# A second `x` buffer in an attention and MLP kernel, and the mixing of a batch spread over three pairs

## The chip, the cores and the metric

The kernel runs on one core of a Trainium2 chip. It is written with five engines in mind: TensorE (PE, matrix products and transposes, with its weight loads shown as PEld), VectorE (DVE), ScalarE (ACT), GpSimd (POOL) and SyncE (SP, which issues all DMAs here). Each engine runs its own queue in order; semaphores order the queues against each other. The metric is the time of one execution on the device in microseconds, as the median of several runs.

## The reference

For each of 4 batches there are 8 heads of attention over 576 positions with a head dimension of 64, in float32:

```python
scores = (q @ k.T) / sqrt(64) + bias          # bias: (8, 576, 576), the same for all batches
attn = exp(scores - max) / (sum + 1e-9)
x[b] = concat over heads of (attn @ v)        # (576, 512)
```

The bias is a small network (hidden size 32, ReLU) of log1p|i - j| / log1p(max(i, 1)). Behind it comes a block on `x`:

```python
h = x.T @ U @ V                # U: 576 x 32, V: 32 x 576: mixes the positions of one batch
u = x + h.T
out = u + relu(u @ w_ch1) @ w_ch2      # w_ch1: 512 x 2048, w_ch2: 2048 x 512
```

The mixing (`x.T @ U @ V`) of a batch needs all heads and all positions of that batch's `x`. The MLP works on `u`, 2304 rows in all.

## The kernel before, in words

Attention runs over 16 pairs: pair p is batch p // 4 and two heads, numbered hp = p % 4. A pair has 9 slots (`slot(p, s)`, lines 504 to 534). Each slot computes one tile of scores, 128 rows by 576 (`scores`: TensorE products `sc`, then a VectorE instruction, line 321, that adds the bias and finds the row minimum), and its exponentials on ScalarE (`exps`, line 340). Slots 3 to 8 and, one pair later, slots 0 and 1 transpose the exponentials on TensorE (`tr`, tile `tb`; `tr_m`, tile `tm`; `tr_mid`, tile `ti`). ScalarE (line 367) or VectorE (line 369) copies each transposed bank into the SBUF tile `pt`: slots 4, 6 and 8 go to ScalarE, 3, 5 and 7 to VectorE, but in pairs with hp = 1 slots 3 and 5 go to ScalarE too (line 520). The PV product of the first half of the rows (`av`, tile `o`, line 423) stands at the end of slot 8; the one of the second half in slot 2 of the next pair. `assemble` transposes the results (tile `tx`) and VectorE writes them, scaled, into `x_sb` (lines 446 and 453): slot 4 of the next pair for the first half, slot 8 for the second.

All transposes and the mixing use PSUM tiles of tag "t". They are one bank each and come in turn from three banks (`psum`, line 77; `rot`, line 716). A use waits until the use three before it has been read out.

`x_sb` holds one batch's `x`, with one buffer. Its mixing runs in the first pair of the next batch whose hp is 1 (pairs 5, 9, 13), because the last `assemble` of the batch is in slot 8 of the pair before:

- `mix_t` (line 457), ahead of slot 0: `mt = U.T x` on TensorE, then `th` on ScalarE and `tl` on VectorE (a sum of two parts in a reduced format).
- `mix_s` (line 484), behind slot 0: `ms` from `th` and `tl`, then `sq` on ScalarE and again on VectorE.
- `mix_h` (line 495), behind slots 1 to 5, for the row blocks 4, 0, 1, 2, 3: a product `mh` with `sq`, a VectorE add into `x_sb` (line 499), and a DMA of the block to `u_dram` (line 500).

The `assemble` of the next batch's first pair in slot 4 writes the same `x_sb`, so it waits until those DMAs have read it. The last batch's mixing (lines 836 to 847) lies between the steps of the MLP.

Three more streams run beside the slots:

- Loads and splits of q and k. `load_pair(p + 2)` is issued on SP at the start of slot 7 into `raw`, which has one buffer. POOL splits it into `hi` and `lo` (lines 155 and 161, four instructions) in slots 2 to 5 of the next pair, for the pair after that.
- The conversion of the 64-bit MLP weights (`conv_ops`, lines 175 to 212; `background`, line 664), one step in each of the slots 0, 1, 2, 6, 7, 8 from pair 2 on: load, two ScalarE steps, two VectorE steps (lines 193 and 199), a join on VectorE (line 205) with an add on POOL (line 210), a store. With three steps a job, and the order fixed, the joins stand in slots 0 and 6 of pairs 3 to 12.
- From pair 13 on the first MLP weights are loaded and split; in slots 6 and 7 of pair 15 `make_ut` adds one use of a "t" bank each (transposes `tu`).

Ahead of all this, a bias phase uses tables in the pool `tabp` (5 KB a partition), which stay allocated until the MLP although nothing reads them after it.

Of the kernel before, what the change touches and what calls it, by code (L numbers as in the profile page):

```python
# [8 lines left out]
F32 = mybir.dt.float32  # L9
F32R = mybir.dt.float32r  # L10
# [8 lines left out]
B, H, S, D = 4, 8, 576, 64  # L19
HP = H // 2  # L20
DM = H * D
# [4 lines left out]
P = 128  # L26
# [20 lines left out]
def kernel(  # L47
# [14 lines left out]
    nc = tc.nc  # L62
# [10 lines left out]
    p0 = ExitStack()  # L73
# [3 lines left out]
    def psum(tag, shape, name):  # L77
        rot[tag].append(rot[tag].pop(0))
        return rot[tag][-1].tile(shape, F32, tag=tag, name=name)
# [7 lines left out]
    p1 = ExitStack()  # L87
    mix = p1.enter_context(tc.tile_pool(name="mix", bufs=1, side="left"))
# [13 lines left out]
    u_sb = mix.tile([P, 5, RANK], F32, name="u_sb")  # L102
    vq = mix.tile([P, 640], F32R, name="vq")
    fold = mix.tile([P, P], F32R, name="fold")
    x_sb = mix.tile([P, 5, DM], F32, name="x_sb")

# [22 lines left out]
    def load_pair(p):  # L131
        b, hp = divmod(p, HP)
        raw = rawp.tile([P, QKW], F32, tag="raw", name="raw")
        nc.sync.dma_start(out=raw[0:D], in_=qk[b, hp])
        nc.sync.dma_start(out=raw[D:P], in_=qk[b, hp])
        qk_ops[p] = raw

    def load_v(p):
        b, hp = divmod(p, HP)
        v_t[p] = vpp.tile([P, 640], F32, tag="v", name="v")  # L140
        nc.sync.dma_start(out=v_t[p], in_=vp[b, hp])
# [70 lines left out]
        return load, [size, low, clamp, shift, join, add], lambda: finish(st["y"].bitcast(F32))  # L212


    tabp = p1.enter_context(tc.tile_pool(name="tabp", bufs=1, side="left"))
    ring = [big.tile([P, 9 * S], F32, tag=f"big{i}", name="ring") for i in (2, 3)]
    ring = [t[:, i * S : (i + 1) * S] for t in ring for i in range(9)]

# [63 lines left out]
            parts = [(bias[hp][t * LEFT : (t + 1) * LEFT, 0:S], bd[4 * P : S, 2 * hp + t, :]) for t in range(2)]  # L282
        return [lambda o=o, i=i: nc.sync.dma_start(out=o, in_=i) for o, i in parts]


    pools = {}

    pair = {}

    def new_pair(p):  # L290
        st = stp.tile([P, 32], F32, tag="st", name="st")
        pair[p] = {"st": st, "P": {}}
# [72 lines left out]
    def copy(eng, out, in_):  # L365
        if eng == "a":
            nc.scalar.copy(out=out, in_=in_)  # L367
        else:
            nc.vector.tensor_copy(out, in_)  # L369
# [64 lines left out]
    def assemble(p, hf):  # L434
        d = pair[p]
        ot = d["ot", hf]
        hp = p % HP
        bank = psum("t", [P, 4, P], "tx")
        o = LEFT if hf == 0 else 0
        for i in range(2):  # L440
            nc.tensor.transpose(bank[:, i, :], ot[:, o + i * P : o + (i + 1) * P], ident)
        if hf == 0:
            nc.tensor.transpose(bank[0:LEFT, 2, :], ot[:, 0:LEFT], ident)
        xs = x_sb[:, 2 * hf : 2 * hf + 2, hp * P : (hp + 1) * P].rearrange("p c (h d) -> p c h d", h=2)
        r = d["st"][:, 21 + 4 * hf : 25 + 4 * hf].rearrange("p (c h) -> p c h", h=2)
        nc.vector.tensor_tensor(
            out=xs,
            in0=bank[:, 0:2, :].rearrange("p c (h d) -> p c h d", h=2),
            in1=r.unsqueeze(3).to_broadcast([P, 2, 2, D]),
            op=ALU.mult,  # L450
        )
        if hf == 0:
            copy("d", x_sb[0:LEFT, 4, hp * P : (hp + 1) * P], bank[0:LEFT, 2, :])
# [2 lines left out]

    def mix_t(b):

        t = psum("t", [P, DM], "mt")
        for c in range(4):  # L460
            mm(
                t[RANK * c : RANK * (c + 1), :],
                lhsT=u_sb[:, c, :],
                rhs=x_sb[:, c, :],
                start=True,
                stop=False,
                tile_position=(0, RANK * c),
            )
        for g in range(4):
            mm(  # L470
                t[RANK * g : RANK * (g + 1), g * P : (g + 1) * P],
                lhsT=u_sb[:, 4, :],
                rhs=x_sb[:, 4, g * P : (g + 1) * P],
                start=False,
                stop=True,
                tile_position=(0, RANK * g),
            )
        th = mix.tile([P, DM], F32R, tag="th", name="th")
        tl = mix.tile([P, DM], F32R, tag="tl", name="tl")
        nc.scalar.copy(out=th, in_=t)  # L480
        nc.vector.tensor_tensor(out=tl, in0=t, in1=th.bitcast(F32), op=ALU.subtract)
        mixt[b] = (th, tl)

    def mix_s(b):

        th, tl = mixt[b]
        s = psum("t", [P, DM], "ms")
        mm(s, lhsT=fold, rhs=th, start=True, stop=False)
        mm(s, lhsT=fold, rhs=tl, start=False, stop=True)
        sq = mix.tile([P, DM], F32R, tag="sq", name="sq")  # L490
        nc.scalar.copy(out=sq, in_=s)
        nc.vector.tensor_tensor(out=sq[D:P], in0=s[D:P], in1=sq[D:P].bitcast(F32), op=ALU.subtract)
        mixt[b] = sq

    def mix_h(b, c):
        n = P if c < 4 else LEFT
        h = psum("t", [P, DM], "mh")
        mm(h, lhsT=vq[:, c * P : (c + 1) * P], rhs=mixt[b], start=True, stop=True)
        nc.vector.tensor_tensor(out=x_sb[0:n, c, :], in0=h[0:n], in1=x_sb[0:n, c, :], op=ALU.add)
        nc.sync.dma_start(out=u_dram[b * S + c * P : b * S + c * P + n, :], in_=x_sb[0:n, c, :])  # L500
# [167 lines left out]
        del queue[:n]  # L668


    pools["pt"] = p1.enter_context(tc.tile_pool(name="ptp", bufs=1, side="left"))
    nc.sync.dma_start(out=ident, in_=ident_in)
    nc.vector.memset(sgn.bitcast(F32), -2.0)
    nc.vector.memset(eps, 1.0e-9)
# [8 lines left out]
    for i in range(len(order) + 2):  # L683
# [23 lines left out]
            load_v({20: 0, 26: 1}[i])  # L707
        if i in early:
            slot(0, early[i])
    nc.vector.memset(x_sb[D:P, 4, :], 0.0)  # L710
    ones = tabp.tile([P, RANK], F32, name="ones")
    nc.vector.tensor_reduce(out=ones, in_=ident.rearrange("p (g r) -> p r g", g=4), op=ALU.add, axis=mybir.AxisListType.X)
    nc.vector.tensor_copy(fold.rearrange("p (g r) -> p g r", g=4), ones.unsqueeze(1).to_broadcast([P, 4, RANK]))
    p0.close()
    psT2 = ctx.enter_context(tc.tile_pool(name="psT2", bufs=2, space=PSUM))
    rot = {"s": [psS], "t": [psT, psT2, psT2]}
    loads[0:0] = bias_loads(3, 0)
# [7 lines left out]
    queue[1:1] = [[]] * 3  # L725

    conv_at = (0, 1, 2, 6, 7, 8)

    def big_views(t, parts):

        views, o = [], 0
        for n, k in parts:
            if k is None:
                o += n
                continue
            views.append(t[:, o : o + n].rearrange("p (k f) -> p k f", k=k) if k else t[:, o : o + n])
            o += n
        return views
# [12 lines left out]
    for p in range(NP):  # L751
        if p > 0:
            new_pair(p)
        if 0 < p < HP - 1:
            bias[p + 1] = big.tile([P, 9 * S], F32, tag=f"big{p + 1}", name=f"bias{p + 1}")
            loads = [o for c in (4, 0, 1, 2, 3) for o in bias_loads(c, p + 1)]
        for s in range(9):
            if s == (1 if p else 0) and p < NP - 1:
                prep = prep_ops(p + 1)
            if s in ((2, 3, 4, 5) if p else (0, 1, 2, 3)) and p < NP - 1:  # L760
                prep.pop(0)()
            if s == 7 and 0 < p < NP - 2:
                load_pair(p + 2)
            if s == 7 and 0 < p < NP - 1:
                load_v(p + 1)
            for o in loads[0:2]:
                o()
            del loads[0:2]
            if p > 0 or s not in early.values():
                if p > HP and p % HP == 1 and s == 0:  # L770
                    mix_t(p // HP - 1)
                slot(p, s)
                background(int(s in conv_at and (p, s) >= CONV_FROM))
                if p > HP and p % HP == 1 and s == 0:
                    mix_s(p // HP - 1)
            if p > HP and p % HP == 1:
                for c in {1: (4,), 2: (0,), 3: (1,), 4: (2,), 5: (3,)}.get(s, ()):
                    mix_h(p // HP - 1, c)
            if p == NP - 3 and s == 1:
                t = big.tile([P, 9 * S], F32R, tag="big0", name="w1q")  # L780
                *wq[0], uth[0] = big_views(t, [(WQ, KD), (WQ, KD), (LINE, None), (UT, KD)])
                feed = first_weights(0)
            if p == NP - 2 and s == 1:
                t = big.tile([P, 9 * S], F32R, tag="big1", name="w2q")
                w2a, w2b, utl[0] = big_views(t, [(WQ, KD), (WQ, KD), (LINE, None), (UT, KD)])
                wq[0] += [w2a, w2b]
                feed = first_weights(1)
            if p == NP - 1 and s == 1:
                t = big.tile([P, 9 * S], F32, tag="big2", name="acc")
                acc.update(enumerate(big_views(t, [(DM, 0)] * 10)))  # L790
                feed = iter(())
            if p >= NP - 3 and s in (1, 2, 4, 5, 7, 8):
                next(feed, None)
            if p == NP - 1 and s in (1, 2, 3, 4, 5):
                load_acc(2 * s - 2)
                load_acc(2 * s - 1)
            if p == NP - 1 and s in (6, 7):
                make_ut(0, s - 6)
# [155 lines left out]
```

## Time and profile before

| what | value |
|---|---|
| median of 3 runs | 774.79 us (770.87 to 774.82) |
| the profiled execution | 773.58 us, of which the span of instructions 771.7 us |
| TensorE busy | 738.4 us (96%) |
| VectorE, ScalarE, POOL busy | 437.4, 361.4, 235.8 us |
| chain that ended last | 72% TensorE |

The span goes from the first to the last instruction of the profiled execution; some 1.9 us of that execution lie outside it. Attention's pairs run from about 60 to 351 us, the MLP behind them. Instructions and stretches are placed by their time from the span's start. In a timeline or a table of stretches, "idle before" in square brackets is the time in which an engine stood still ahead of an instruction, with the instruction that ended it.

### The profile page before, as it was taken

The page shows a single profiled execution, that of the slowest core. Times are in us where ns is not written, and L with a number is a line of the kernel's source. Part 1 is how long each engine was busy: PE and PEld are TensorE (multiplying, and loading weights), DVE is VectorE, ACT ScalarE, POOL GpSimd, SP SyncE. Part 2 cuts the span into 40 slices and gives each one's busy share as a digit, 9 for nine tenths or more (in the row PEclk, how much of TensorE's full clock was granted, in tenths as well). Part 3 has the DMA queues.
Part 4 walks back from the last instruction along what each step waited for, and adds up shares of the span by engine and source line. Part 5 has one row for each costly group of instructions (what it writes and reads, how often), then busy time and mean ns, then how long its engine had stood idle before and what let it go on. Part 6 is the DMA issues. An engine that isn't in the chain of part 4 may idle for free.

```text
span 771.7 us, 13867 instructions
## 1 busy us (share of the span) xinstructions
PE 738.4 (96%) x5348; PEld 613.5 (80%) x5348; DVE 437.4 (57%) x949; ACT 361.4 (47%) x807; POOL 235.8 (31%) x225
## 2 busy tenths in 40 slices
PE   6989899999999998999999999999999999999998
PEld 4436777677867776878888889988998999999986
DVE  8995468868877885663439734762247722221222
ACT  7996577777777775774125513431114410111010
POOL 0004456655665566630005502540015500000000
PEclk9999999999999999999999999999999999999999
DMA  7898994465455546550063301320002200001111
GB/s 212 252 319 268 241 275 123 122 178 127 124 158 151 123 97 176 153 168 1 21 205 98 109 1 42 96 83 1 1 26 85 69 1 1 1 28 56 55 42 68
DMA packets 39377, 84.01 MB, mean 109 GB/s; under 512 B 6800, under 2 KB 9488, under 8 KB 37264
## 3 DMA queue, kind: packets, MB, share of 16 engines
q1 hardware_dynamic: 39312, 83.13, 37.0%
q8 instruction: 42, 0.69, 0.4%
q14 instruction: 23, 0.19, 0.1%
HBM read 60.96 MB, written 22.15 MB: 108 GB/s over the span
## 4 chain that ended last, share of the span: by engine, by line
PE 72%; ACT 8%; DVE 6%; DMA 5%; POOL 4%; issue 3%; SPq 1%; DVEq 0%; POOLq 0%; ACTq 0%
PE po L606 24%; PE ph L583 23%; PE o L423 8%; PE sc L319 7%; PE tb L387 4%; DMA raw<-in_qk_dram 3%; ACT ring L244 2%; DVE wt L205 1%; ACT ring L266 1%; PE bs L255 1%; POOL hi L161 1%; POOL lo L161 1%; DVE p L321 1%; POOL hi L155 1%; ACT p L340 1%
## 5 line engine op out<-in xcount | busy, mean ns | idle before, releaser
L588 ACT ACTIVATE hh<-ph 128x1024 fp32r<-128x1024 f32 x36 | 36.9, 1026 | 205.3 <-PE ph L583 205.3
L589 DVE SCALAR_TENSOR_TENSOR hh<-ph,hh 128x1024 fp32r<-128x1024 f32 x36 | 44.1, 1224 | 141.1 <-ACT hh L588 141.1
L340 ACT ACTIVATE p<-p,st 128x576 f32<-128x576 f32 x128 | 99.8, 780 | 41.3 <-DVE st L321 41.2
L210 POOL TENSOR_TENSOR wy<-wt,wy 128x256 int32<-128x256 int32 (+1 forms) x68 | 50.2, 738 | 217.8 <-DVE wt L205 195.9
L321 DVE CUSTOM_DVE_ANT_0 p<-sc,bias 128x576 f32<-128x576 f32 x128 | 95.9, 749 | 31.8 <-PE sc L319 26.6
L606 PE MATMUL po<-w2q,hh 128*128 128x512 f32 x432 | 101.8, 391 | 1.5 <-DVE acc L609 1.5
L606 PE MATMUL po<-wq,hh 128*128 128x512 f32 x432 | 103.2, 395 | 0.0
L319 PE MATMUL sc<-hi 128*128 128x288 f32 x320 | 101.6, 333 | 1.3 <-DVE st L321 0.8
L583 PE MATMUL ph<-ut,w1q 128*128 128x256 f32 x768 | 94.2, 280 | 0.0
L606 PEld LDWEIGHTS po<-w2q,hh 128*128 128x128 f32 x432 | 79.9, 188 | 17.9 <-issue 1.9
L606 PEld LDWEIGHTS po<-wq,hh 128*128 128x128 f32 x432 | 80.1, 188 | 17.6
L423 PE MATMUL o<-pt,v 128*64 128x320 f32 (+1 forms) x640 | 91.7, 412 | 2.1 <-ACT pt L367 2.1
L319 PE MATMUL sc<-lo,hi 128*128 128x288 f32 x320 | 90.7, 299 | 3.0 <-POOL lo L161 3.0
L583 PEld LDWEIGHTS ph<-ut,w1q 128*128 128x128 f32 x768 | 92.1, 188 | 1.5 <-issue 0.6
L583 PEld LDWEIGHTS ph<-ut,wq 128*128 128x128 f32 x768 | 90.3, 188 | 1.4
L583 PE MATMUL ph<-ut,wq 128*128 128x256 f32 x768 | 90.6, 277 | 0.0
L609 DVE TENSOR_TENSOR acc<-po,acc 128x512 f32<-128x512 f32 x72 | 49.6, 689 | 72.4 <-PE po L606 72.3
L387 PE MATMUL tb<-ident,p 128*128 128x128 f32 x512 | 78.2, 276 | 5.8 <-DVE x_sb L369 4.2
L423 PEld LDWEIGHTS o<-pt,v 128*64 128x64 f32 x640 | 45.2, 136 | 37.6 <-ACT pt L367 7.0
L319 PEld LDWEIGHTS sc<-hi 128*128 128x128 f32 x320 | 61.2, 191 | 15.1 <-issue 8.6
L387 PEld LDWEIGHTS tb<-ident,p 128*128 128x128 f32 x512 | 61.9, 142 | 8.3 <-issue 6.2
L155 POOL TENSOR_SCALAR hi<-raw 128x1216 fp32r<-128x1216 f32 x30 | 36.3, 1210 | 99.8 <-DMA raw<-in_qk_dram 90.6
(99 smaller groups left out, 1036.9 us busy)
## 6 DMA issues: line engine op xcount, KB each, us to landing
raw<-in_qk_dram SPq DMA_DIRECT2D x31, 608.0 KB, 7.9
wraw<-in_w_ch_dram SPq DMA_DIRECT2D x64, 256.0 KB, 2.6
bias_dram<-ring SPq DMA_DIRECT2D x36, 288.0 KB, 4.1
v<-in_vp_dram SPq DMA_DIRECT2D x16, 320.0 KB, 8.3
bias<-bias_dram SPq DMA_DIRECT2D x16, 288.0 KB, 4.5
acc<-u_dram SPq DMA_DIRECT2D x18, 256.0 KB, 4.9
out_dram<-acc SPq DMA_DIRECT2D x18, 256.0 KB, 2.0
bias<-bias_dram SPq DMA_DIRECT2D x16, 256.0 KB, 4.7
```

Source lines behind the costliest of these rows:

```text
L155: nc.gpsimd.tensor_scalar(out=hi[:, a:e], in0=raw[:, a:e], scalar1=1.0, scalar2=0.0, op0=ALU.mult, op1=ALU.add)
L210: nc.gpsimd.tensor_tensor(out=st["y"], in0=st["t"], in1=st["y"], op=ALU.add)
L319: mm(ps[:, a, 0:HALF], lhsT=hi[:, q0 : q0 + P], rhs=kk, start=(i == 0), stop=(i == n - 1))
L321: nc.vector.tensor_tensor_reduce(out=halves(dst), in0=ps[:, :, 0:HALF], in1=halves(bias[hp][:, s * S : (s + 1) * S]), scale=-0.125, scalar ...
L340: nc.scalar.activation(out=dst, in_=dst, func=AF.Exp, bias=st[:, s : s + 1], scale=-1.0, accum_out=st[:, 10 + s : 11 + s])
L387: nc.tensor.transpose(bank[:, kb, :], src[:, b0 + kb * P : b0 + (kb + 1) * P], ident)
L423: mm(o[hd * D : (hd + 1) * D, 0:n], lhsT=v[:, vb * D : (vb + 1) * D], rhs=pt[:, pb, :], start=(j == 0), stop=(j == 4),)
L583: mm(st["ps"][:, f, :], lhsT=w, rhs=u[:, k, :], start=(i == 0), stop=(i == 3 * KD - 1))
L588: nc.scalar.activation(out=hh[n], in_=st["ps"], func=AF.Relu)
L589: nc.vector.scalar_tensor_tensor(out=hl[n], in0=st["ps"], scalar=0.0, in1=hh[n].bitcast(F32), op0=ALU.max, op1=ALU.subtract)
L606: mm(ps, lhsT=h, rhs=w, start=(m == 0), stop=(m == 3 * FG - 1))
L609: nc.vector.tensor_tensor(out=a, in0=ps, in1=a, op=ALU.add)
```

## The change

`x` gets a second buffer. The list `xbuf` holds both; batch b uses `xbuf[b % 2]`. Its space is that of the bias tables: their pool `tabp` now belongs to the part that is closed after the bias phase, the pool `ptp` of the transposed exponentials is opened ahead of it, and the new pool `xp` takes the freed place. The rows of the new buffer that no batch writes are set to zero once. `sq` shares the place of `th`.

With the second buffer, the mixing of a batch no longer has to be finished before slot 4 of the pair it starts in. `mix_t` stays ahead of slot 0 of pairs 5, 9, 13; `mix_s` goes behind slot 2 of that pair, and the five `mix_h` behind slot 7 of that pair, slots 2 and 7 of the next, and slots 2 and 7 of the one after. The last batch's mixing is left where it was.

```diff
--- before.py
+++ after.py
@@ -102,7 +102,7 @@
     u_sb = mix.tile([P, 5, RANK], F32, name="u_sb")
     vq = mix.tile([P, 640], F32R, name="vq")
     fold = mix.tile([P, P], F32R, name="fold")
-    x_sb = mix.tile([P, 5, DM], F32, name="x_sb")
+    xbuf = [mix.tile([P, 5, DM], F32, name="x_sb")]
 
 
 
@@ -212,7 +212,8 @@
         return load, [size, low, clamp, shift, join, add], lambda: finish(st["y"].bitcast(F32))
 
 
-    tabp = p1.enter_context(tc.tile_pool(name="tabp", bufs=1, side="left"))
+    pools = {"pt": p1.enter_context(tc.tile_pool(name="ptp", bufs=1, side="left"))}
+    tabp = p0.enter_context(tc.tile_pool(name="tabp", bufs=1, side="left"))
     ring = [big.tile([P, 9 * S], F32, tag=f"big{i}", name="ring") for i in (2, 3)]
     ring = [t[:, i * S : (i + 1) * S] for t in ring for i in range(9)]
 
@@ -282,8 +283,6 @@
             parts = [(bias[hp][t * LEFT : (t + 1) * LEFT, 0:S], bd[4 * P : S, 2 * hp + t, :]) for t in range(2)]
         return [lambda o=o, i=i: nc.sync.dma_start(out=o, in_=i) for o, i in parts]
 
-
-    pools = {}
 
     pair = {}
 
@@ -434,7 +433,8 @@
     def assemble(p, hf):
         d = pair[p]
         ot = d["ot", hf]
-        hp = p % HP
+        b, hp = divmod(p, HP)
+        x_sb = xbuf[b % 2]
         bank = psum("t", [P, 4, P], "tx")
         o = LEFT if hf == 0 else 0
         for i in range(2):
@@ -456,6 +456,7 @@
 
     def mix_t(b):
 
+        x_sb = xbuf[b % 2]
         t = psum("t", [P, DM], "mt")
         for c in range(4):
             mm(
@@ -487,13 +488,14 @@
         s = psum("t", [P, DM], "ms")
         mm(s, lhsT=fold, rhs=th, start=True, stop=False)
         mm(s, lhsT=fold, rhs=tl, start=False, stop=True)
-        sq = mix.tile([P, DM], F32R, tag="sq", name="sq")
+        sq = mix.tile([P, DM], F32R, tag="th", name="sq")
         nc.scalar.copy(out=sq, in_=s)
         nc.vector.tensor_tensor(out=sq[D:P], in0=s[D:P], in1=sq[D:P].bitcast(F32), op=ALU.subtract)
         mixt[b] = sq
 
     def mix_h(b, c):
         n = P if c < 4 else LEFT
+        x_sb = xbuf[b % 2]
         h = psum("t", [P, DM], "mh")
         mm(h, lhsT=vq[:, c * P : (c + 1) * P], rhs=mixt[b], start=True, stop=True)
         nc.vector.tensor_tensor(out=x_sb[0:n, c, :], in0=h[0:n], in1=x_sb[0:n, c, :], op=ALU.add)
@@ -668,7 +670,6 @@
         del queue[:n]
 
 
-    pools["pt"] = p1.enter_context(tc.tile_pool(name="ptp", bufs=1, side="left"))
     nc.sync.dma_start(out=ident, in_=ident_in)
     nc.vector.memset(sgn.bitcast(F32), -2.0)
     nc.vector.memset(eps, 1.0e-9)
@@ -707,11 +708,13 @@
             load_v({20: 0, 26: 1}[i])
         if i in early:
             slot(0, early[i])
-    nc.vector.memset(x_sb[D:P, 4, :], 0.0)
+    nc.vector.memset(xbuf[0][D:P, 4, :], 0.0)
     ones = tabp.tile([P, RANK], F32, name="ones")
     nc.vector.tensor_reduce(out=ones, in_=ident.rearrange("p (g r) -> p r g", g=4), op=ALU.add, axis=mybir.AxisListType.X)
     nc.vector.tensor_copy(fold.rearrange("p (g r) -> p g r", g=4), ones.unsqueeze(1).to_broadcast([P, 4, RANK]))
     p0.close()
+    xbuf.append(p1.enter_context(tc.tile_pool(name="xp", bufs=1, side="left")).tile([P, 5, DM], F32, name="x_sb"))
+    nc.vector.memset(xbuf[1][D:P, 4, :], 0.0)
     psT2 = ctx.enter_context(tc.tile_pool(name="psT2", bufs=2, space=PSUM))
     rot = {"s": [psS], "t": [psT, psT2, psT2]}
     loads[0:0] = bias_loads(3, 0)
@@ -725,6 +728,7 @@
     queue[1:1] = [[]] * 3
 
     conv_at = (0, 1, 2, 6, 7, 8)
+    mix_at = {(1, 7): 4, (2, 2): 0, (2, 7): 1, (3, 2): 2, (3, 7): 3}
 
     def big_views(t, parts):
 
@@ -767,15 +771,15 @@
                 o()
             del loads[0:2]
             if p > 0 or s not in early.values():
-                if p > HP and p % HP == 1 and s == 0:
-                    mix_t(p // HP - 1)
+                b, hp = divmod(p, HP)
+                if b and (hp, s) == (1, 0):
+                    mix_t(b - 1)
                 slot(p, s)
                 background(int(s in conv_at and (p, s) >= CONV_FROM))
-                if p > HP and p % HP == 1 and s == 0:
-                    mix_s(p // HP - 1)
-            if p > HP and p % HP == 1:
-                for c in {1: (4,), 2: (0,), 3: (1,), 4: (2,), 5: (3,)}.get(s, ()):
-                    mix_h(p // HP - 1, c)
+                if b and (hp, s) == (1, 2):
+                    mix_s(b - 1)
+                if b and (hp, s) in mix_at:
+                    mix_h(b - 1, mix_at[hp, s])
             if p == NP - 3 and s == 1:
                 t = big.tile([P, 9 * S], F32R, tag="big0", name="w1q")
                 *wq[0], uth[0] = big_views(t, [(WQ, KD), (WQ, KD), (LINE, None), (UT, KD)])
```

## Rows read from the trace of the kernel before

**Rows 1.** The page's busy times, TensorE's entry (first of its line).
```profile
PE 738.4 (96%) x5348; PEld 613.5 (80%) x5348; DVE 437.4 (57%) x949; ACT 361.4 (47%) x807; POOL 235.8 (31%) x225
```

**Rows 2.** Stretches of pairs 5, 7, 8, 9, 11, 13: length, busy by engine, clock, DMA.
```profile
139.97:163.30 23.33, 19.92 (x150) 15.21 (x149) 18.48 (x45) 15.51 (x38) 16.35 (x14) 1.00 0.53 148
...
180.04:197.98 17.94, 16.97 (x128) 13.29 (x127) 14.85 (x40) 12.82 (x33) 10.17 (x9) 1.00 0.53 132
197.98:214.51 16.53, 16.53 (x128) 13.28 (x127) 12.85 (x36) 12.94 (x33) 9.67 (x8) 1.00 0.56 144
214.51:236.41 21.90, 19.58 (x150) 14.90 (x150) 16.93 (x45) 15.45 (x37) 14.16 (x10) 1.00 0.58 162
...
252.94:270.71 17.77, 16.90 (x127) 13.21 (x127) 14.69 (x38) 12.82 (x33) 9.35 (x9) 1.00 0.55 134
...
287.45:311.86 24.41, 20.67 (x150) 16.25 (x149) 14.65 (x38) 15.55 (x36) 15.68 (x11) 0.93 0.61 172
```

**Rows 3.** Waits of the whole span: total us, times, longest.
```profile
DVE x_sb L446 <- DMA u_dram<-x_sb: 6.0, 4, 2.3
...
PE mh L498 <- DVE sq L492: 4.2, 3, 1.5
PE tb L387 <- DVE x_sb L369: 4.2, 2, 2.4
```

**Rows 4.** Timeline of pair 5's mixing: start, length, engine, line, tile, [idle before].
```profile
142.81 0.41 PEld L461 LDWEIGHTS mt<-x_sb,u_sb 128*32 128x32 f32 x8 [0.49 <-DVE st L321]
...
149.89 0.47 PE L498 MATMUL mh<-sq,vq 128*128 128x512 f32 x1 [1.51 <-DVE sq L492]
...
153.13 0.50 PE L498 MATMUL mh<-sq,vq 128*128 128x512 f32 x1
...
153.47 0.29 PE L319 MATMUL sc<-hi 128*128 128x288 f32 x1
...
158.63 0.63 PE L387 MATMUL tb<-ident,p 128*128 128x128 f32 x4 [1.74 <-DVE x_sb L369]
```

**Rows 5.** Groups by line, VectorE, 130 to 300 us: busy us, mean ns.
```profile
L205 DVE SCALAR_TENSOR_TENSOR wt<-wraw,sgn,wt 128x256 int32<-128x256 int32 (+1 forms) x17 | 15.9, 936 | 0.3
...
L499 DVE TENSOR_TENSOR x_sb<-mh,x_sb 128x512 f32<-128x512 f32 (+1 forms) x11 | 7.5, 679 | 1.9 <-PE mh L498 1.9
```

**Rows 6.** Timeline of pair 7, slots 6 to 8.
```profile
196.75 0.49 DVE L205 SCALAR_TENSOR_TENSOR wt<-wraw,sgn,wt 128x256 int32<-128x256 int32 x1
...
197.45 0.60 PE L387 MATMUL tb<-ident,p 128*128 128x128 f32 x4
...
197.95 0.69 DVE L369 COPY pt<-tb 128x512 f32<-128x512 f32 x1
```

**Rows 7.** Timeline of pair 15, slot 7's copy and slot 8's transposes.
```profile
346.73 0.68 DVE L369 COPY pt<-tb 128x512 f32<-128x512 f32 x1
...
347.56 0.63 PE L387 MATMUL tb<-ident,p 128*128 128x128 f32 x4 [0.92 <-DVE pt L369]
```

**Rows 8.** Timeline of pair 6, slots 6 to 8, with POOL.
```profile
178.71 2.79 POOL L161 TENSOR_TENSOR lo<-raw,hi 128x1216 fp32r<-128x1216 f32 x1
178.80 2.97 DVE L205 SCALAR_TENSOR_TENSOR wt<-wraw,sgn,wt 128x256 int32<-128x256 int32 x1
...
179.51 0.60 PE L387 MATMUL tb<-ident,p 128*128 128x128 f32 x4
...
182.49 0.69 DVE L369 COPY pt<-tb 128x512 f32<-128x512 f32 x1
```

**Rows 9.** Timeline of the loads of `raw` (SP) and POOL's first split.
```profile
144.66 0.47 SPq L134 DMA_DIRECT2D raw<-in_qk_dram  x1
...
191.52 1.21 POOL L155 TENSOR_SCALAR hi<-raw 128x1216 fp32r<-128x1216 f32 x1 [2.51 <-DMA raw<-in_qk_dram]
...
217.42 0.47 SPq L134 DMA_DIRECT2D raw<-in_qk_dram  x1
```

**Rows 10.** Timeline of VectorE at pair 0's end.
```profile
69.06 0.76 DVE L321 CUSTOM_DVE_ANT_0 p<-sc,bias 128x576 f32<-128x576 f32 x1 [3.60 <-DMA bias<-bias_dram]
```

## The prediction

> **What bounds the kernel now.** I read the page's engine lines first, then the stretches by pair, the waits, and the timeline around the mixing. TensorE is busy for 96% of the span [rows 1], so time can be won only where it stands still or runs slowly. The change touches pairs 4 to 15. In the stretches, each cut from one pair's first PV product (slot 8) to the next pair's, a pair without mixing can run with no hole at all: pair 8 takes 16.53 us and TensorE is busy 16.53 us of it. The pairs that carry the mixing of the batch before (5, 9, 13) take 23.33, 21.90 and 24.41 us with 19.92, 19.58 and 20.67 us busy [rows 2]. The holes have two names in the waits: the first `mh` product waits for VectorE's `sq` (4.2 us in three), and slot 5's transposes wait for VectorE's copy into `x_sb` (4.2 us in two), which stands behind a wait for the transfer `u_dram<-x_sb` (6.0 us in four) [rows 3]. Pair 5's timeline shows both: 1.51 us ahead of the first `mh`, 1.74 us ahead of the `tb` transposes at 158.63 [rows 4]. That second wait is one for a PSUM bank. Transposes and mixing share three banks used in turn (tag "t"); with an `mh` put between, slot 5's transposes get the bank of `tx` three uses earlier, which VectorE had not emptied.
>
> **What the change takes away.** Mixing costs TensorE 19.58 - 16.53 = 3.05 us a batch wherever it stands [rows 2]; that moves and does not go. The holes of the mixing pairs are 3.41 + 2.32 + 3.74 = 9.47 us. The wait of the first mixing matmul for the last `assemble`, 0.49 us [rows 4], stays in each, since `mix_t` stays. `mix_s` goes two slots later and the first `mix_h` five slots after it, so `sq` is ready; `assemble` writes the other buffer, whose transfer left a batch ago. I take 9.47 - 1.5 = 8.0 us away. In pair 13 the granted clock was 0.93, part of the pair at 1.2 instead of 2.4 GHz, after a hole; the same matmuls took 20.67 instead of 19.58 us [rows 2]. If the hole goes, 1.1 us goes with it. Together 9.1 us.
>
> **What it adds.** Per batch, slot 2 of two pairs gets one `mh` behind its PV. VectorE is busy 12.85 of 16.53 us in pair 8 [rows 2] and gets no scores while that PV runs, so the add of 679 ns [rows 5] fits: cost 0, at most the add, 0.7 us each. `mix_h` also goes behind slot 7 in three pairs (5, 6, 7 and so on). There it uses one bank between slot 7's transposes and slot 8's two uses. Before, slot 8's `tb` takes the bank of slot 6's `ti`; after, it takes the bank of slot 7's `tb`, which VectorE copies. In pair 7 slot 8's `tb` started at 197.45, and that copy ended at 197.95 + 0.69 = 198.64 [rows 6]: today PV starts after the `tb` and covers VectorE's lag, then PV would have to queue behind it. Pair 15 shows the price already, because its slot 7 has one more bank use (`make_ut`): the copy ended at 347.41, the `tb` started at 347.56 after a wait of 0.92 us for it [rows 7]. So the stall in an undisturbed pair is 198.64 + 0.15 - 197.45 = 1.34 us, less the 0.34 us by which the `mh` itself delays TensorE (153.13 to 153.47 [rows 4]): 1.0 us. Six pairs (5, 6, 7, 9, 10, 11): 6.0 us.
>
> Ahead of that copy VectorE has the conversion's join (line 205), due in slot 6. In pair 7 it took 0.49 us [rows 6]. In pair 6 it came 0.09 us behind POOL's `lo` of 2.79 us and ended just after it, 2.97 us long, and the copy started 2.98 us after the `tb` that would have to wait for it [rows 8]. So each of the six stalls grows by 0 to 2.5 us. Between 130 and 300 us the 17 joins took 15.9 us [rows 5]; at 0.49 each that is 7.6 us too many, nine of the joins stand in slot 6, 0.85 us each. I take that mean: 6 x 0.85 = 5.1 us. The Trainium skill (SBUF — State Buffer, section SBUF: two separate sides) says why: a GpSimd instruction and a VectorE one with two SBUF inputs share a port pair that the first holds to its end. By it alone, with joins at random in a POOL round of 18.2 us (below) that holds two instructions of 2.79 and two of 1.21 us, I estimate 0.5 us a join, and the sum would come out 2 us lower; the trace's mean is higher, since slot 6 meets POOL's work more often than by chance.
>
> Pairs 13 to 15 have no joins: 1.0 less the join's 0.49, 0.5 us each, and pair 15, where the `make_ut` use pushes one wait more onto the add, another 0.7: 2.2 us. The mixing pairs keep their copies of slots 3 and 5 on ScalarE, which is busy 15.45 us in pair 9 [rows 2]; packed closer, ScalarE may lag, from 0 to 1.5 us in each of 5, 9 and 13. A late TensorE finds VectorE caught up and stalls less in slot 8, so I add nothing.
>
> One thing comes back. Pairs 7 and 11 took 17.94 and 17.77 us against 16.53 [rows 2], because VectorE entered them late after its blocked join. If TensorE has waited in slot 8 before, that lag is paid already: 1.4 + 1.2 = 2.6 us less.
>
> **The rest at nothing.** The second buffer's memset must wait for the last reader of the bias tables, on VectorE with pair 0's scores queued behind it; a few us later VectorE waits 3.60 us for a bias load anyway [rows 10], which hides it. If that cover were gone, the price is below 1 us. `sq` in `th`'s place waits for products that it needs anyway. The moved DMAs stand on SP behind the loads of slot 7, and nobody reads `u_dram` of a batch before the MLP's loads in pair 15. The moved pool `ptp` only shifts addresses. The last batch's mixing is as before.
>
> **The sum** on the profiled execution (771.7 us span, 773.58 us in all): 773.58 - 9.1 - 2.6 + 6.0 + 5.1 + 2.2 = 775.2. The median of the three runs, 774.79, lies 1.2 above that execution, so 776.4 us. With no join blocked it is 771.3, with four of the six blocked for 2.5 us 781.3: the forecast's own range. The change would trade holes in three pairs for smaller ones in nine.
>
> **Rivals.**
> (a) The third bank is free in time, and the holes simply go: 774.8 - 9.1 = 765.7. For it: VectorE has one thing less to do in the mixing pairs. Against it: pair 15's wait [rows 7], and no pair in rows 6 to 8 whose copy was done before the `tb`.
> (b) As (a), but the loop of loads and splits then sets the pace. `raw` has one buffer: POOL waits for the transfer (2.51 us at 191.52), splits, and only then the next load is issued. Four rounds, from the issue at 144.66 to that at 217.42, took 72.8 us, 18.2 each [rows 9]. A batch's four pairs would need 4 x 16.53 + 3.05 + 0.5 = 69.7 us. If the rounds stay as they are, 3.1 us of each batch's gain are lost, 7.6 us over two and a half batches: 773.3. If they tighten with the pairs (SP holds an issue back behind a join), nothing is: 765.7. I put it at 769.5. For it: POOL waits for the transfer. Against it: in the forecast TensorE is late enough to hide the loop.
> (c) Slower: the joins meet POOL in most pairs. POOL's phase follows the loop, not TensorE, so the pairs can lock into it. Each blocked join costs 2.5 us in slot 8, as in pair 6 [rows 8]; from three of six on the loss passes 0.5% (6.0 + 7.5 + 2.2 - 11.7 = +4.0). Five of six, with three drops of the clock at 1.1 us after holes of some 3 us, give 774.8 + 9 + 3.3 = 787. Against it: the 7.6 us too many of the 17 joins [rows 5] are three full ones, no more.
> (d) The holes stay, because the mixing still waits (for the transfer, or for `sq`): 774.8. Against it: two buffers, and a batch between the uses of one.
>
> **How the numbers follow.** Forecast 0.57, (a) 0.06, (b) 0.14, (c) 0.18, (d) 0.05. A measurement of this kernel tells about 0.5% (3.9 us) from no change. Faster by more than that (below 770.9): (a), over half of (b), little of the forecast: 0.18. Slower by more (above 778.7): (c) and the forecast's upper end: 0.25. Within: 0.57. The range that leaves out 2 in 10 goes from 768.5 to 783.5.
>
> **What the changed profile would show.** Right: no wait of `mh` for `sq`, none of `x_sb` for `u_dram`; pairs 5, 9, 13 at about 19 to 21 us; in pairs 5, 6, 7, 9, 10, 11 a wait of slot 8's `tb` for VectorE's `pt` copy (line 369), 1.0 us where the join took 0.5 us and up to 3.5 where it took 3; pairs 7 and 11 not shorter than before. Wrong: no such wait (then (a) or (b), told apart by scores that wait for POOL's `lo`), or joins near 3 us in most pairs (c). Wrong at the root if slot 8's `tb` waits for another bank than slot 7's.

## The result, and the profile after

The changed kernel took 784.16 us (median of four, 782.76 to 786.72) against 774.81 us beside it: a ratio of the means of 1.0134, 95% interval 1.0086 to 1.0181. That is 1.3% slower, clear of the noise, where the forecast was 776.4, and 0.7 us above the end of the range. The profiled execution took 782.85 us, its span 780.8 us, 9.1 more than before. By the last PV product of attention the difference is 8.6 us already (356.72 against 348.12 us), so the loss lies in the pairs.

Stretches of the changed kernel, cut as in [rows 2] (length, busy time of each engine, granted clock, DMA): pairs 5 to 13.
```profile
139.70:161.16 21.46, 20.14 (x146) 14.54 (x145) 17.20 (x42) 16.55 (x42) 15.29 (x13) 1.00 0.46 116
161.16:181.31 20.15, 17.70 (x130) 13.83 (x129) 15.64 (x39) 13.31 (x34) 11.86 (x10) 0.98 0.55 145
181.31:203.22 21.91, 19.23 (x129) 14.07 (x128) 16.54 (x39) 12.83 (x33) 10.50 (x8) 0.94 0.50 130
203.22:219.74 16.52, 16.52 (x128) 13.27 (x127) 11.46 (x33) 11.80 (x30) 9.27 (x7) 1.00 0.55 141
219.74:240.51 20.77, 19.89 (x147) 14.40 (x146) 16.25 (x42) 16.24 (x41) 11.84 (x10) 1.00 0.51 131
240.51:259.60 19.09, 17.23 (x130) 13.63 (x129) 14.29 (x39) 13.06 (x34) 10.60 (x8) 1.00 0.55 145
259.60:278.38 18.78, 17.23 (x129) 13.61 (x128) 14.87 (x39) 13.05 (x34) 10.62 (x8) 1.00 0.57 151
278.38:298.68 20.30, 18.78 (x128) 14.89 (x127) 15.05 (x36) 11.83 (x31) 10.43 (x8) 0.92 0.54 128
298.68:318.77 20.09, 19.45 (x146) 14.23 (x145) 12.17 (x33) 15.45 (x37) 10.36 (x9) 1.00 0.36 102
```

The kernel before has this row for pair 12, which neither kernel gives any mixing.
```profile
270.71:287.45 16.74, 16.70 (x127) 13.29 (x126) 13.54 (x37) 12.95 (x33) 9.67 (x8) 1.00 0.48 111
```

The mixing pairs (first, fifth, last row) are shorter: 62.32 us together against 69.64 in [rows 2]. All pairs between them but pair 8 are longer, and pairs 6, 7 and 12 have a granted clock below 1. Pair 12 went from 16.74 to 20.30 us without one new instruction in it.

TensorE's waits from 130 to 360 us in the changed kernel (total, times, longest):
```profile
PE tb L386 <- DVE pt L368: 8.3, 7, 2.4
PE tb L386 <- DVE x_sb L501: 1.5, 2, 1.3
PE sc L318 <- DVE st L320: 1.1, 1, 1.1
```
The two waits of [rows 3] that the change was to end, `mh` for `sq` and `x_sb` for `u_dram`, are gone. The first row is slot 8's `tb`, as forecast.

Timeline of the end of pair 6 (start, length, engine, line; idle before in brackets):
```profile
176.94 1.91 DVE L205 SCALAR_TENSOR_TENSOR wt<-wraw,sgn,wt 128x256 int32<-128x256 int32 x1
...
179.56 0.69 DVE L368 COPY pt<-tb 128x512 f32<-128x512 f32 x1
...
180.39 0.98 PE L386 MATMUL tb<-ident,p 128*128 128x128 f32 x4 [2.35 <-DVE pt L368]
```
This is the forecast's stall: a held join, the copy of slot 7 behind it, then slot 8's `tb`. Right after the 2.35 us the four transposes take 0.98 us instead of 0.60 [rows 6]: the granted clock from 180.39 to 181.31 is 0.57, so part of them ran at the lower clock. Pair 8, which gets no `mix_h` and so keeps the old turn of the banks, has a held join in the same slot and no wait of slot 8's `tb`:
```profile
218.50 2.05 DVE L205 SCALAR_TENSOR_TENSOR wt<-wraw,sgn,wt 128x256 int32<-128x256 int32 x1
...
219.21 0.60 PE L386 MATMUL tb<-ident,p 128*128 128x128 f32 x4
```

Timeline of slots 2 to 4 of pair 7:
```profile
190.40 1.22 POOL L155 TENSOR_SCALAR hi<-raw 128x1216 fp32r<-128x1216 f32 x1
190.51 1.25 DVE L193 TENSOR_SCALAR wt<-wt 128x256 f32<-128x256 f32 x1 [0.64 <-ACT wt L187]
191.70 2.78 POOL L161 TENSOR_TENSOR hi<-raw,hi 64x1216 fp32r<-64x1216 f32 x1
...
191.79 2.83 DVE L199 TENSOR_SCALAR wt<-wt 128x256 int32<-128x256 int32 x1
...
194.55 0.68 DVE L501 TENSOR_TENSOR x_sb<-mh,x_sb 128x512 f32<-128x512 f32 x1
...
195.37 0.63 PE L386 MATMUL tb<-ident,p 128*128 128x128 f32 x4 [1.29 <-DVE x_sb L501]
```
Here is what the forecast did not have. The conversion's clamp and shift of slot 2 (lines 193 and 199, 0.3 us each when free) each start about 0.1 us behind a POOL instruction and end with it. VectorE leaves slot 2 some 3.5 us late, and the add behind it keeps the bank that slot 4's `tb` needs.

The same happens in slot 2 of pair 12, but there no mixing stands and no bank has a new turn:
```profile
287.49 2.78 POOL L161 TENSOR_TENSOR hi<-raw,hi 64x1216 fp32r<-64x1216 f32 x1
287.59 2.83 DVE L199 TENSOR_SCALAR wt<-wt 128x256 int32<-128x256 int32 x1
...
291.15 0.40 PE L318 MATMUL sc<-hi 128*128 128x288 f32 x1 [1.08 <-DVE st L320]
```
Here TensorE waits for VectorE at the scores (the minimum of line 320), not at a "t" bank, and from 291.15 to 296 us its granted clock is 0.71.

### The profile page after: what moved, and what is told of

The parts are those of the page before. It is cut to its first block, busy times and chain, and to the rows that moved or that the text cites. A ratio compares the mean times of both kernels' runs of the same rounds, so it can differ in the third digit from the quotient of the medians.

```text
span 780.8 us, 13883 instructions
## 1 busy us (share of the span) xinstructions
PE 743.9 (95%) x5348; PEld 612.7 (78%) x5348; DVE 445.5 (57%) x950; ACT 361.3 (46%) x807; POOL 235.5 (30%) x225
## 4 chain that ended last, share of the span: by engine, by line
PE 64%; DVE 12%; ACT 8%; DMA 5%; POOL 5%; issue 4%; SPq 1%; DVEq 0%; POOLq 0%; ACTq 0%
PE po L608 23%; PE ph L585 23%; PE o L422 7%; PE sc L318 4%; DVE p L320 3%; PE tb L386 3%; DMA raw<-in_qk_dram 2%; ACT ring L245 2%; ACT p L339 2%; DVE pt L368 2%; DVE wt L205 2%; DVE ring L247 2%; POOL hi L161 1%; POOL lo L161 1%; POOL hi L155 1%
## 5 line engine op out<-in xcount | busy, mean ns | idle before, releaser
L422 PE MATMUL o<-pt,v 128*64 128x320 f32 (+1 forms) x640 | 94.8, 417 | 1.2 <-ACT pt L366 1.0
L318 PEld LDWEIGHTS sc<-lo,hi 128*128 128x128 f32 x320 | 61.1, 191 | 4.5 <-POOL lo L161 3.6
```

Source lines behind the costliest of these rows:

```text
L318: mm(ps[:, a, 0:HALF], lhsT=hi[:, q0 : q0 + P], rhs=kk, start=(i == 0), stop=(i == n - 1))
L422: mm(o[hd * D : (hd + 1) * D, 0:n], lhsT=v[:, vb * D : (vb + 1) * D], rhs=pt[:, pb, :], start=(j == 0), stop=(j == 4),)
```

## The experiments

The theory after the result: VectorE's conversion steps are held by POOL's splits; this was so before too, but the new use of the "t" banks lets VectorE's lateness through to TensorE. The rivals: the second buffer itself; the bank stall and the clock without POOL; VectorE's load as such. Ratios are to the kernel before, run beside each.

| kernel | median us | ratio | 95% interval |
|---|---|---|---|
| buffer only | 767.2 | 0.9923 | 0.9894 to 0.9952 |
| `mix_h` ahead of slot 7 | 780.51 | 1.0085 | 1.0057 to 1.0113 |
| changed, steps left out | 766.77 | 0.9925 | 0.9897 to 0.9953 |
| before, steps left out | 770.74 | 0.9978 | 0.9959 to 0.9998 |
| changed, `mh` in PV's bank | 766.18 | 0.9913 | 0.9886 to 0.9939 |
| changed, steps moved | 767.55 | 0.9941 | 0.9919 to 0.9964 |
| PV's bank and steps moved | 764.65 | 0.9904 | 0.9880 to 0.9929 |
| all mixing in PV's bank | 781.95 | 1.0122 | 1.0093 to 1.0152 |
| changed, clamp out of slot 2 | 777.8 | 1.0085 | 1.0055 to 1.0115 |
| changed, join out of slot 6 | 776.56 | 1.0052 | 1.0024 to 1.0080 |
| before, steps moved | 771.9 | 1.0004 | 0.9985 to 1.0024 |

**The buffer alone.**
```diff
-    mix_at = {(1, 7): 4, (2, 2): 0, (2, 7): 1, (3, 2): 2, (3, 7): 3}
+    mix_at = {(1, 1): 4, (1, 2): 0, (1, 3): 1, (1, 4): 2, (1, 5): 3}
...
-                if b and (hp, s) == (1, 2):
+                if b and (hp, s) == (1, 0):
                     mix_s(b - 1)
```


> The second buffer is kept, the mixing goes back to the places it had before (mix_s behind slot 0, the five mix_h behind slots 1 to 5 of pairs 5, 9 and 13). Theory: what made the changed kernel slower is the place of the mixing products (the mix_h behind slot 7 shifts the turn of the three banks, and what follows from that), not the buffer. Then the waits for u_dram (6.0 us in four before) are gone, the wait of the first mix_h for sq (4.2 us in three) stays, slot 8's tb waits for no pt copy in pairs 6, 7, 10 and 11, these four pairs take 16.5 to 18.0 us as before, and the kernel takes 768 to 773 us. Rival: the second buffer itself costs (its place in memory, its memset, sq in the place of th): then 778 us or more with the schedule of before.

767.2 us, just under the expected range. TensorE's waits in the kernel with the buffer alone:
```profile
PE mh L500 <- DVE sq L493: 4.2, 3, 1.5
...
PE tb L386 <- DVE pt L368: 0.9, 1, 0.9
```
The wait for `sq` stayed, those for the transfer went, pairs 6, 7, 10 and 11 took 17.30, 16.99, 16.56 and 16.73 us. The buffer alone is a gain; the new places of the mixing are what lost it.

**`mix_h` ahead of slot 7.**
```diff
+                if b and s == 7 and (hp, s) in mix_at:
+                    mix_h(b - 1, mix_at[hp, s])
                 slot(p, s)
...
-                if b and (hp, s) in mix_at:
+                if b and s != 7 and (hp, s) in mix_at:
```


> As the changed kernel, but the mix_h of slot 7 is issued ahead of the slot and not behind it. Slot 8's tb then takes the bank of that mix_h, whose add stands on VectorE ahead of the copy of slot 7's tb. Theory (bank stall): the waits of slot 8's tb for the pt copy (8.3 us in seven) fall to 2 us or less in all, TensorE is not late any more in pairs 6, 7, 10 and 11, its granted clock does not drop there (0.98, 0.94 and 0.92 in pairs 6, 7 and 12), and the kernel takes 766 to 775 us. Rival 1 (the mix_h of slot 2, or POOL's split that meets the conversion's steps, costs by itself): the slot-8 waits go and pairs 7 and 12 still take 20 us or more, 777 to 781 us. Rival 2 (the mixing anywhere near slot 8 costs, through VectorE's add): the wait only changes its name, 782 us or more.

780.51 us; TensorE's longest sum of waits in this kernel:
```profile
PE tb L386 <- DVE x_sb L501: 8.3, 6, 2.6
```
My theory expected under 2 us and fell here; the second rival was right on the wait, though its 782 us was too much. The wait changed its name and kept its 8.3 us: the add, like the copy, stands on VectorE behind the joins. Which of the two VectorE instructions empties the bank made no difference. Pairs 7 and 12 stayed at 21.26 and 20.27 us, as the first rival had it.

**Without VectorE's conversion steps**, in both kernels.
```diff
...
-            groups += [[size, low], [clamp, shift], [join, add]]
+            bare = 4 <= i and len(ops) > 16 and src0
+            groups += [[size, low], [] if bare else [clamp, shift], [add] if bare else [join, add]]
...
-    queue += pipeline(jobs)
+    queue += pipeline(jobs, True)
```


> The changed kernel without VectorE's three conversion steps (clamp, shift, join) for the 16 weight jobs that run beside attention: these steps are left out of the computation, ScalarE's and POOL's steps and all transfers stay. Theory (POOL's splits block VectorE's conversion steps, and that is the term that I missed): pairs 7 and 12 fall from 21.9 and 20.3 us to 18 or less, slot 8's waits fall to about 1 us each or less, and the kernel takes 766 to 772 us, within 3 us of the kernel before with the same steps left out. Rival (bank stall and clock alone): the waits and the clock drops stay, it remains 7 us or more above the kernel before with the same steps left out.

> The kernel before without VectorE's clamp, shift and join for the 16 weight jobs beside attention (left out of the computation). Theory: in the kernel before these steps cost little, the 2.6 us of pairs 7 and 11 and part of the holes of pairs 5 and 9, so 768 to 772 us. Rival: they cost the kernel before as much as the changed one, 763 to 767 us, and then the port is not what sets the two kernels apart.

766.77 and 770.74 us. The two kernels change places; they lie 4.0 us apart, where at most 3 were expected. Pairs 7 and 12 of the changed kernel without the steps:
```profile
177.31:195.16 17.85, 17.35 (x129) 13.64 (x128) 11.74 (x33) 13.06 (x34) 10.97 (x10) 1.00 0.61 163
...
266.63:283.36 16.73, 16.69 (x128) 13.29 (x127) 10.15 (x30) 12.04 (x31) 10.21 (x8) 1.00 0.48 122
```
The same steps cost the kernel before 0.2% and the changed one about 2% (1.0134 against 0.9925). This takes the work away too, so it doesn't tell work from holding.

**`mix_h` in the bank of the PV product.**
```diff
-        h = psum("t", [P, DM], "mh")
+        h = psA.tile([P, 512], F32, tag="a", name="mh") if b < B - 1 else psum("t", [P, DM], "mh")
...
-    mix_at = {(1, 7): 4, (2, 2): 0, (2, 7): 1, (3, 2): 2, (3, 7): 3}
+    mix_at = {(1, 4): 4, (1, 6): 0, (2, 4): 1, (2, 6): 2, (3, 4): 3}
```


> As the changed kernel, but the mix_h products of the first three batches go to the bank of the PV product (tag a, idle between slots 2 and 8) and no more to the three t banks; they stand behind slots 4 and 6 of the first two pairs and slot 4 of the third (with tag a they can't stand behind slot 2 or 7, where PV has the bank). mix_t and mix_s stay as changed. Theory: VectorE's lateness reaches TensorE only through the turn of the t banks; with that as before, slot 8's tb waits for VectorE in no pair without mixing (0 to 1 us in all instead of 8.3), pairs 6, 7, 10, 11 and 12 take 16.7 to 18.2 us although they carry the same adds and the same conversion steps, the granted clock stays at 0.99 or more in each, and the kernel takes 762 to 768 us: the 767.2 us of the kernel with the buffer alone less the 4.2 us of waits for sq. Rival: VectorE has simply too much to do, or POOL's splits hold it wherever the adds stand; then these pairs stay near 19 to 21 us and the kernel at 776 us or more.

766.18 us, with the steps where they were. VectorE's lines of the steps from 130 to 300 us in this kernel (busy us, mean ns):
```profile
L205 DVE SCALAR_TENSOR_TENSOR wt<-wraw,sgn,wt 128x256 int32<-128x256 int32 (+1 forms) x18 | 15.9, 885 | 0.3
L193 DVE TENSOR_SCALAR wt<-wt 128x256 f32<-128x256 f32 (+1 forms) x17 | 11.0, 646 | 5.3 <-ACT wt L187 5.3
L199 DVE TENSOR_SCALAR wt<-wt 128x256 int32<-128x256 int32 (+1 forms) x17 | 6.3, 372 | 0.6
```
33.2 us together. The same three lines of the changed kernel:
```profile
L205 DVE SCALAR_TENSOR_TENSOR wt<-wraw,sgn,wt 128x256 int32<-128x256 int32 (+1 forms) x17 | 14.1, 832 | 0.3
L199 DVE TENSOR_SCALAR wt<-wt 128x256 int32<-128x256 int32 (+1 forms) x17 | 12.0, 705 | 0.6
L193 DVE TENSOR_SCALAR wt<-wt 128x256 f32<-128x256 f32 (+1 forms) x17 | 8.7, 510 | 5.3 <-ACT wt L187 5.3
```
34.8 us. VectorE is held nearly as long in both, and the one is 2% faster: how long it is held in all does not decide. What differs beside the bank is which step is held. The shift (line 199) took at most 0.71 us in this kernel, 2.83 us twice in the changed one. The edit also moved the adds to other slots, so it does not tell the bank from the place. One part of the expectation failed: pairs 10 and 11 took 19.59 and 18.80 us, after one wait of 2.2 us of PV for an add of its bank, with the clock at 0.91 in pair 11 (its profiled execution, 769.76 us, was the longest of the six).

**The steps in other slots**, in the changed kernel, with the last edit, and in the kernel before.
```diff
-    queue[1:1] = [[]] * 3
+    queue[1:1] = [[]]
...
-    conv_at = (0, 1, 2, 6, 7, 8)
+    conv_at = {6: 1, 7: 1, 8: 2, 0: 1, 1: 1}
...
-                background(int(s in conv_at and (p, s) >= CONV_FROM))
+                background(conv_at.get(s, 0) if (p, s) >= CONV_FROM else 0)
```


> As the changed kernel with its bank turn, but the conversion's steps on VectorE are issued in slots 7, 8, 0 and 1 (before: 8, 0, 2 and 6), away from slots 2 to 6 in which POOL splits the next q and k. The same work is done. Theory: what costs is that these steps meet POOL's splits, not that VectorE does them; slot 8's stall is then as in the kernel with the steps left out (1.9 us in five), pairs 7 and 12 take under 19 us, and the kernel takes 768 to 777 us. Rival: the steps' own time on VectorE ahead of the copies is what costs, wherever they stand: 781 us or more.

> Both of the last two: mix_h in the bank of the PV product and the conversion's VectorE steps in slots 7, 8, 0 and 1. Theory: with the turn of the banks as before VectorE's lateness is hidden already, so the second edit adds little: 760 to 767 us, within 3 us of the kernel with the PV bank alone. Rival (POOL's meeting the steps costs by itself, banks or not): 5 us or more below that kernel.

> The kernel before, with the conversion's VectorE steps in slots 7, 8, 0 and 1 as in the run that took 767.55 us. Theory: before the change a held step costs TensorE little, as with the steps left out (770.74 us): 768 to 772 us, that is 1 to 4 us of gain against 16.6 us in the changed kernel. Rival: the edit is worth as much here (760 us or less), and then the change itself is neutral to it.

767.55, 764.65 and 771.9 us. The changed kernel with the steps moved, its wait and its pairs 7 and 12:
```profile
PE tb L386 <- DVE pt L368: 1.8, 5, 0.4
```
```profile
178.03:195.88 17.85, 17.36 (x129) 13.66 (x128) 13.31 (x39) 13.26 (x33) 10.57 (x8) 1.00 0.60 163
...
267.35:284.08 16.73, 16.69 (x128) 13.29 (x127) 11.99 (x35) 12.29 (x30) 10.09 (x8) 1.00 0.54 127
```
All the work is done and the span is 15.3 us shorter (765.5 against 780.8); the three lines take 18.6 us instead of 34.8. In the kernel before the same edit is worth nothing (1.0004). So the new places of the mixing cost little when no step is held, and the steps cost little with the old places or with `mh` in PV's bank: there moving them gains 0 to 2 us. With the new places it gains some 15.

Two things work together here, and the rows tell them apart. A held join of slot 6 costs nothing without the new turn of the banks (pair 8), and up to 2.4 us with it (pair 6). The hold of slot 2 costs without a new turn too (pair 12); it does not occur in the kernel before, nor with the buffer alone, nor with `mh` in PV's bank (shift 0.71 us at most between 130 and 300 us in each). By the rows, the new places bring it about by shifting the pairs against POOL's splits. The combination of both edits has the lowest median, 764.65 us; its interval overlaps those of the two single edits, so it is not shown to beat them.

**All mixing in PV's bank.**
```diff
-        t = psum("t", [P, DM], "mt")
+        t = psA.tile([P, DM], F32, tag="a", name="mt") if b < B - 1 else psum("t", [P, DM], "mt")
...
+    mix_at = {(1, 7): 4, (2, 4): 0, (2, 6): 1, (3, 4): 2, (3, 6): 3}
```


> All mixing products of the first three batches (mix_t, mix_s, mix_h) in the PV product's bank: mix_t behind slot 3, mix_s behind slot 5 and one mix_h behind slot 7 of the first pair, mix_h behind slots 4 and 6 of the second and third. The t banks' turn is that of a pair without mixing everywhere. Theory: mixing then costs little more than its 3.05 us of products per batch: pairs 5 to 7 together within 4 us of three plain pairs, 758 to 766 us. Rival: the one PV bank becomes the wait (each mixing step waits for the copy or add of the one before it, and slot 8's PV for the add behind slot 7): waits of 1 to 3 us per pair, 768 us or more.

781.95 us: the rival was right. TensorE's first wait in this kernel, and its pair 6:
```profile
PE o L422 <- DVE x_sb L501: 7.6, 4, 2.5
```
```profile
163.44:185.64 22.20, 20.63 (x128) 14.64 (x129) 15.70 (x36) 11.90 (x30) 10.49 (x8) 0.87 0.45 115
```
PV of slot 8 waits for the add behind slot 7, and the clock falls to 0.87: the same fault on another bank.

**Each collision by itself.** These are two kernels; both call `background` as in the edit that moves the steps.
```diff
+    conv_at = {0: 2, 1: 1, 6: 1, 7: 1, 8: 1}   # clamp and shift out of slot 2
+    conv_at = {0: 1, 1: 1, 2: 1, 7: 2, 8: 1}   # join out of slot 6
```


> As the changed kernel, but the two conversion steps of slot 2 (clamp and shift) are issued in slot 1, their ScalarE steps in slot 0; the join of slot 6 stays. Theory: in pairs 7 and 12 POOL's split held these two steps for 4.1 us and that was the term missing in the prediction; these pairs fall under 19 us, the waits of slot 8's tb behind the join stay at 5 to 9 us in all, and the kernel takes 774 to 780 us, near the forecast of 776.4. Rival: the loss is all from the join of slot 6, so this edit gives under 3 us: 781 us or more.

> As the changed kernel, but the join of slot 6 is issued in slot 7, behind the copy of slot 7's tb; the clamp and shift of slot 2 stay. Theory: slot 8's tb waits 2 us or less in all for the pt copy (the bank turn alone), TensorE is not late, so POOL's split comes later in the pair and the steps of slot 2 are held less as well: 768 to 775 us. Rival: slot 2's steps are held as before in pairs 7 and 12 (over 20 us each), 777 us or more.

777.8 and 776.56 us. With the clamp out of slot 2, TensorE's waits are
```profile
PE tb L386 <- DVE pt L368: 7.3, 7, 1.8
PE o L422 <- ACT pt L366: 5.1, 9, 0.6
```
and pair 12 takes 17.38 us, but pair 7 still 19.87: the join's stall is left, and PV now waits 5.1 us in all for ScalarE, whose steps moved as well (0.3 us in the changed kernel). With the join out of slot 6, slot 8's wait is 1.9 us as without any steps, but the shift is held in four pairs running, 9 to 12, of which the timeline shows:
```profile
223.75 2.85 DVE L199 TENSOR_SCALAR wt<-wt 128x256 int32<-128x256 int32 x1
...
243.69 2.83 DVE L199 TENSOR_SCALAR wt<-wt 128x256 int32<-128x256 int32 x1
...
263.60 2.85 DVE L199 TENSOR_SCALAR wt<-wt 128x256 int32<-128x256 int32 x1
...
283.54 2.83 DVE L199 TENSOR_SCALAR wt<-wt 128x256 int32<-128x256 int32 x1
```
They are 19.9 us apart, and pairs 10 and 11 take 19.92 us each: the pairs run in step with POOL's rounds. The theory's expectation for this run (768 to 775) missed, since it had the slot-2 hold follow from the stall of slot 8; it can stand without it. The rival missed too: pairs 7 and 12 took 17.85 and 18.68 us. The spans of the four kernels, 780.8 with both collisions, 774.3 and 775.2 with one, 765.5 with none, make both together worth 15.3 us. Parted, slot 6 is worth 8.8 us alone and 5.6 beside slot 2, slot 2 9.7 alone and 6.5 beside slot 6. These parts are rough: the 774.3 has the waits for ScalarE in it, and in the 775.2 other pairs are held than in the changed kernel.

## Why the prediction was wrong

**Right: the holes.** 8.0 us of holes and 1.1 us of clock were forecast to go. With no step held, pairs 5, 9 and 13 take 20.33, 19.62 and 20.10 us with 19.93, 19.40 and 19.47 us busy: 1.25 us of holes are left of 9.47, and the clock of pair 13 is 1.00. In the changed kernel itself 2.84 us are left.

**Right: the bank stall. Right in part by luck: the base of the sum.** Slot 8's `tb` waits for slot 7's copy in all six pairs named. Pair 7 waits 1.0 us with a join of 0.48 us ahead, as worked out from [rows 6], and 0.4 without the join; pair 9, its join also free, waits 0.6. The forecast with no join held was 773.58 - 9.1 - 2.6 + 6.0 + 2.2 = 770.1 on the profiled run. Moving the steps also takes the six free joins (0.5 each) out of these stalls: 767.1. Its profiled execution took 767.38 us. Two errors cancel in this. That sum has 5.2 us of stalls in slot 8, and the trace has 1.8. Against it, TensorE is busy 3.6 us longer in pairs 6, 7, 10, 11, 14 and 15, which got the `mix_h`, but only 1.4 us less in the mixing pairs, 1.1 of which the forecast had put down to the clock: mixing did not move at the same price.

**About right, too dear: the held joins of slot 6.** In the six pairs the joins took 6.1 us, 3.2 above 0.48 each, where I had 5.1; the stall in all was 8.3 us.

**Wrong: "cost 0" for slot 2, and POOL left where it was.** This is the step that failed. I priced the add of slot 2 with VectorE free there, and took from [rows 5] and [rows 8] that what POOL holds is the join of slot 6. The sum had nothing for lines 193 and 199 and nothing for pair 12, which gets no mixing. These steps are equally exposed once POOL's first split reaches slot 2. It starts 9.1 us into pair 7 after, 11.5 us before [rows 9], and 7.8 us into pair 12 after, 11.9 before. Pair 7 took 4.06 us more than with the steps moved, pair 12 3.57; less pair 7's free join of 0.5, this is 7.1 of the 7.65 us between 775.2 and 782.85. "A late TensorE finds VectorE caught up and stalls less" looked at slot 8 alone: a late TensorE also meets POOL elsewhere in the pair.

The Trainium skill (SBUF — State Buffer, section SBUF: two separate sides) names both kinds of VectorE instruction that contend with POOL, those with two SBUF inputs and those in a two-port mode; I applied the first only. The trace fits the second: one-input steps of 1.25 and 2.83 us beside POOL's 1.22 and 2.78; their mode itself no row shows.

**The clock** was in rival (c) only. Pairs 6, 7 and 12 were busy 17.70, 19.23 and 18.78 us, against 17.33, 17.36 and 16.69 with the steps moved: 4.3 us for the same products. Not all of it is the clock: with the join out of slot 6, pair 10 is busy 18.09 us at a clock of 1.00, where the steps moved give 17.23. That run lets the clock be priced in pair 12, which has the same two holds there (1.24 and 2.83 us) and the same wait at the scores, and a clock of 1.00:
```profile
274.33:293.01 18.68, 17.16 (x127) 13.29 (x126) 15.36 (x36) 12.27 (x31) 10.29 (x8) 1.00 0.43 102
```
The holds took 1.95 us of this (16.73 with the steps moved); in the changed kernel, at 0.92, the pair took another 1.62. No run changed the clock by itself, so this is read from the rows, not shown by an experiment.

Of the rivals, (c) was the mechanism in kind: conversion steps meeting POOL in one pair after another, with drops of the clock. It had 0.18, was priced at 787, and looked only at the joins.

Why POOL's split moves to slot 2 can be read from the trace. Before, POOL stood still until its load had landed: 2.51 us in pair 7 [rows 9], 4.08 in pair 12, 17.3 us in seven waits between 130 and 300 us. In the changed kernel these waits are 1.9 us in four, none of them in pairs 7 and 12. Their loads are issued 1.9 and 2.4 us ahead of the start of the pair's stretch, where before they came 2.3 and 2.6 us into it. So the split follows POOL's instruction ahead of it (line 359) at once, in slot 2, where the clamp and the shift stand. It comes as early in pairs 10 and 11 (8.4 and 8.0 us into them), but there the clamp had started 0.1 us ahead of it or more, and the shift too in pair 10; only the shift of pair 11 was held, for 1.18 us. So it hangs on tenths of a microsecond which step is caught. Rival (b) had it that a late TensorE hides the loop of loads, but not what that does to the splits. Delaying the split was not tried, so this too is read, not shown by an experiment.

## What to carry to other kernels

Before adding a use to a set of banks taken in turn, list which engine empties the bank that each later use will now get, and how late that engine is already: lateness that cost nothing can become a wait of the bounding engine. An engine that is 57% busy can be late at one place in every round, and a shift in phase can move that place, so every instruction that another engine can hold has to be priced, in every round and also where the change puts nothing, not only the one held today. When a change that should gain loses, try keeping it and moving its neighbours: here that turned 1.0134 into 0.9941 without touching the change.

## What was not expected of the hardware

VectorE's one-input steps over 128x256 elements (0.29 us) were held to 1.25 and 2.83 us, to the end of a POOL instruction that had started about 0.1 us earlier. Holding can lock in: with the join out of slot 6 the shift took 2.83 to 2.85 us in four pairs running, 19.9 us apart.
